# Retention heads and a routed MoE on one core: the load of k, its cast, and the order of 1956 operations

## The chip, the core and the metric

One core of one Trainium2 chip runs the whole program. The metric is device time in microseconds (us) of one execution, lower is better. TensorE is called PE below, VectorE DVE, ScalarE ACT, GpSimd POOL and SyncE SP, as in the profile.

## What is computed

Eight batches of eight heads, 576 positions, head size 64. The scores are masked by a decay that is a power of the distance; the outputs of all heads form 4608 rows of 512, which a router sends to two of eight experts each.

```python
scores = scale * np.matmul(q, k.transpose(0, 1, 3, 2))
Dmat = np.where(rel >= 0, gamma[:, None, None] ** rel[None, :, :], 0.0)
ret = scores * Dmat[None, :, :, :]
x = np.matmul(ret, v)                      # rows of 512 after a transpose
noisy_logits = x @ w_gate + np.log1p(np.exp(x @ w_noise)) * noise
top2 = np.argpartition(-noisy_logits, 2, axis=1)[:, :2]
out[mask] += top2_w[mask, k, None] * (np.maximum(x[mask] @ w1[e], 0.0) @ w2[e])
```

All inputs and the output are f32; the matmuls run in bf16.

## The kernel before, in words

**Units.** The attention part is cut into 16 units (`NU`), each of four heads (`hq`) of one batch (`b` within the pair `bp`), for the first 512 positions. The last 64 positions of a pair of batches are the tail (`load_tail` L652, `tail` L827). For a unit, `load` (L621) issues the DMAs of k, q and v; `cast` (L663) scales q (L676) and v (L683) by the decay tables on DVE or POOL and writes bf16; `tr` (L692) transposes K (L710) and Q (L704) on PE and has ACT or DVE copy them out of PSUM (helper `copy`, L450 on ACT, L452 on DVE); `scores` (L717) multiplies (L736) and masks on DVE (L744); `states` (L751) forms k times v per block (L769), copied by ACT into `tb`; `out_` (L784) adds both parts (L804, L814) and writes xT. After each fourth unit come a tail and `route` (L895): logits (L922), top 2 by a chain of small DVE operations, ranks (L985, L987), a table of row numbers (L1036), and the rows of x with their weights stored to the DRAM buffer xd (L1072).

**How k arrives.** In `load`, k is taken by a DMA that POOL issues (L647, `nc.gpsimd`), which casts f32 to bf16 on the way, into the class of buffers `kb`: eight bf16 pieces of the SBUF tile `ws[2]` that will hold expert 2's weights later. q comes as f32 on SP's queue (L635) into four pieces of `ws[1]` (class `wq`), v as f32 on SP's queue into `big`. K's transposes and the states read the k buffer directly, through `keys` (L689).

```python
go = nc.gpsimd if n == "k" else nc.sync
...
pl.cls("kb", [(ws[2][:, i * F:(i + 1) * F], None) for i in range(8)])
pl.cls("wq", [(ws[1][:, 2 * i * F:2 * (i + 1) * F].bitcast(F32), None) for i in range(4)])
```

The router's two weight matrices and the noise (`later`, L581) are issued on ACT's queue at the program's start (L589, L602, L606).

**Experts.** Weights of experts 0, 1 and 2 are cast by DMAs that POOL issues (L1112, L1116); those of the others come as f32 on SP's queue into `big` and are cast by ACT or DVE (L450, L452). Experts 1 and 2 share memory with q and k, so their weights wait until these buffers are done with. Rows of an expert are gathered from xd in tiles of 128 by POOL (L1179). 15 tiles can start before the last route, from the rows that the first three routes have filled; they go through `up` (L1261, 256 columns at a time) and `second` (L1349) and are called early tiles here. The other tiles wait for the fourth route; they go through `wide` (L1287, up to 512 columns) with the second layer of the tile before woven in (L1349). ReLU (L1270, L1272) and the scaling by the router's weight (L1397 on ACT, L1399 on DVE) empty PSUM; POOL scatters the rows to the output (L1405). For the wide tiles a small DVE copy takes the weight and the row number out of the gathered rows (L1212, `pl`).

**What sets the order.** `record` lists all operations with what they read and write. `Plan.run` (L274) then goes through them with a greedy rule: among the operations whose buffers and inputs are there, it takes the one with the smallest key of planned start, priority and number; where two engines can do an operation it chooses by planned end. The priorities are those of the code plus an entry of the table `ORDER` by name and stage. Each engine executes its instructions in the order that results. For PE's planned idle time in the attention part, `run` puts in matmuls without use (`warm`, L458).

```python
key = (round(t * 20), o.prio, o.i)
if pick is None or key < pick[0]:
    pick = (key, o, e, t, c, taken)
```

## Time and profile before

| what | value |
|---|---|
| three runs | 417.48, 423.11, 436.01 us (median 423.11) |
| profiled execution | 420.08 us |
| its span, first to last instruction | 418.5 us |
| busy over the span | PE 378.8, DVE 166.6, ACT 255.2, POOL 302.1 us |
| bytes moved by DMA | read 72.97 MB, written 26.36 MB |
| first scores (L736) | 13.41 us |
| last scores (L736) | 134.90 us |
| fourth route table (L1036) | 166.69 us |
| first wide matmul (L1287) | 193.28 us |
| PE's last wide and second-layer work | about 409.5 us |

The span has two halves. Up to about 193 us PE works on attention, routes and early tiles; after it on the wide tiles alone. "Busy" is the time in which an engine executes something; PEclk is the share of TensorE's full clock that was granted; the DMA share adds up the time of the packets of 16 DMA engines, and passes 1 where two queues have packets in flight on one engine at a time.

### The profile page before, as it was taken

The numbers are of one execution on the slowest core, as the hardware profiler recorded it, in microseconds if no ns is written. First come the engines' busy times: TensorE is split into PE (matmuls) and PEld (weight loads), VectorE is DVE, ScalarE is ACT, GpSimd is POOL, SyncE is SP. The second block draws the span as 40 slices with busy tenths as digits, with TensorE's granted clock in tenths as the row PEclk, the third lists the DMA queues.
The fourth block names the chain that finished last, engine by engine and source line by source line (L and its number), as shares of the span: only waits on it lengthen the run. The fifth ranks groups of instructions, "written<-read, shape, count | busy, mean of one in ns | idle before, by whom it ended". The sixth has DMA issues, their size and how long they took to land. (4 is left out here: it accounts for less than half of the span.)

```text
span 418.5 us, 11275 instructions
## 1 busy us (share of the span) xinstructions
PE 378.8 (91%) x4415; PEld 235.4 (56%) x4415; DVE 166.6 (40%) x512; ACT 255.2 (61%) x432; POOL 302.1 (72%) x333
## 2 busy tenths in 40 slices
PE   5779786959989889999999999999999999999991
PEld 2457665837768667775566544544554554454461
DVE  5856578694979959220224322113112101100001
ACT  1437676746778765555567777756675676554550
POOL 8997766696399746776577767787786687753882
PEclk9999899697999969999999999999999999999997
DMA  9998999999995999579999999999999999991894
GB/s 219 266 235 189 259 228 186 296 260 257 256 231 107 257 237 254 151 177 238 243 342 383 270 259 279 239 278 223 289 236 232 183 268 182 214 152 25 130 127 105
DMA packets 112584, 93.75 MB, mean 224 GB/s; under 512 B 65807, under 2 KB 89872, under 8 KB 112530
## 3 DMA queue, kind: packets, MB, share of 16 engines
q0 software_dynamic: 34512, 40.31, 52.5%
q1 hardware_dynamic: 75330, 52.53, 49.5%
q8 instruction: 35, 0.57, 0.6%
q10 hardware_dynamic: 2688, 0.18, 0.5%
q14 instruction: 19, 0.16, 0.2%
HBM read 72.97 MB, written 26.36 MB: 237 GB/s over the span
## 5 line engine op out<-in xcount | busy, mean ns | idle before, releaser
L1349 PE MATMUL ps<-W,half 128*128 128x512 bf16 x568 | 185.1, 381 | 0.0
L1287 PE MATMUL ps<-big,W 128*128 128x512 bf16 (+4 forms) x640 | 180.6, 329 | 0.0
L1270 ACT ACTIVATE half<-ps 128x512 bf16<-128x512 f32 (+5 forms) x186 | 93.1, 506 | 77.0 <-PE ps L1287 64.0
L1179 POOL DMA_INDIRECT xg<-xd,xi x80 | 84.9, 1061 | 36.8 <-issue 15.0
L1405 POOL DMA_INDIRECT out_dram<-half,pl x59 | 79.8, 1352 | 28.4 <-ACT half L1270 13.9
L1287 PEld LDWEIGHTS <-W 128*128 128x128 bf16 x640 | 62.6, 98 | 48.7 <-issue 1.0
L1349 PEld LDWEIGHTS <-half 128*128 128x128 bf16 x568 | 55.2, 98 | 60.3 <-issue 0.6
L1212 DVE COPY pl<-xg 128x3 f32<-128x3 f32 (+1 forms) x65 | 13.4, 207 | 117.6 <-DMA xg<-xd,xi 117.5
L744 DVE TENSOR_TENSOR half<-ps,mask 128x512 bf16<-128x512 f32 x64 | 40.4, 683 | 16.0 <-PE ps L736 9.9
L450 ACT ACTIVATE half<-ps 128x1024 bf16<-128x1024 bf16 (+1 forms) x36 | 35.0, 992 | 14.5 <-PE ps L1201 6.0
L683 POOL TENSOR_TENSOR half<-big,tab 128x512 bf16<-128x512 f32 x30 | 31.9, 1080 | 7.2 <-DMA big<-in_v_dram 4.4
L450 ACT ACTIVATE W<-big 128x1024 bf16<-128x1024 f32 x34 | 35.5, 1051 | 0.0
L1261 PE MATMUL ps<-half,W 128*128 128x256 bf16 (+1 forms) x288 | 31.1, 263 | 0.1
L450 ACT ACTIVATE tb<-ps 64x512 bf16<-64x512 f32 x32 | 18.9, 592 | 18.3 <-PE ps L769 18.1
L1397 ACT ACTIVATE half<-ps,pl 128x512 f32<-128x512 f32 x42 | 28.7, 682 | 0.1
L1399 DVE TENSOR_SCALAR half<-ps,pl 64x256 f32<-64x256 f32 (+1 forms) x21 | 11.9, 570 | 39.3 <-PE ps L1368 21.3
L1405 POOL DMA_INDIRECT out_dram<-half,xg x15 | 15.4, 1026 | 16.7 <-ACT half L1397 11.5
L1261 PEld LDWEIGHTS <-W 128*128 128x128 bf16 x288 | 24.6, 101 | 4.7 <-issue 0.2
L676 POOL TENSOR_TENSOR half<-W,tabq 128x1024 bf16<-128x1024 f32 x11 | 20.9, 1903 | 5.4 <-DMA W<-in_q_dram 4.4
L450 ACT ACTIVATE xT<-ps 128x512 bf16<-128x512 f32 (+1 forms) x39 | 19.7, 555 | 6.2 <-PE ps L885 4.2
L458 PE MATMUL ps<-mask,ident__61 128*128 128x512 bf16 x67 | 18.3, 403 | 5.2 <-DVE wgn L592 5.2
L769 PE MATMUL ps<-half,W 64*64 64x64 bf16 (+2 forms) x512 | 18.8, 220 | 3.1 <-issue 2.4
(181 smaller groups left out, 425.1 us busy)
## 6 DMA issues: line engine op xcount, KB each, us to landing
big<-in_moe_w_dram SPq DMA_DIRECT2D x40, 512.0 KB
W<-in_q_dram SPq DMA_DIRECT2D x32, 256.0 KB
big<-in_v_dram SPq DMA_DIRECT2D x14, 512.0 KB
W<-in_moe_w_dram POOLq DMA_DIRECT2D x12, 512.0 KB, 13.0
xd<-xg SPq DMA_DIRECT2D x16, 264.0 KB
W<-in_k_dram POOLq DMA_DIRECT2D x14, 256.0 KB, 10.2
xg<-xd,xi POOLq DMA_INDIRECT x80, 7.2
big<-in_v_dram SPq DMA_DIRECT2D x4, 256.0 KB
```

Source lines behind the costliest of these rows:

```text
L450: self.nc.scalar.activation(out, in_, Act.Copy)
L676: self.eng(e).tensor_tensor(o, i, tabq.t[:, 2 * hq:2 * hq + 2].unsqueeze(3).to_broadcast([P, 2, 8, HD]), Alu.mult)
L683: self.eng(e).tensor_tensor(o, i, t, Alu.mult)
L744: nc.vector.tensor_tensor(S.t.bitcast(BF16).rearrange("p (h c x) -> p h c x", h=2, c=2)[:, h], p[h].t.rearrange("p (c x) -> p c x", c=2), ...
L769: nc.tensor.matmul(o[h * HD:(h + 1) * HD, hp, n, :], lhsT=self.keys(kn, hq, c, r, 2 * hp + h)[:k], rhs=vv[:k, r, c, y].unsqueeze(1).to_bro ...
L1179: ins = nc.gpsimd.indirect_dma_start(out=x.t[:n, :], out_offset=None, in_=self.xd[:rows, :], in_offset=IOff(ap=xi.t[:n, h:h + 1], axis=0), ...
L1261: nc.tensor.matmul(pv()[:, f2, :], lhsT=w.t[:, o:o + P], rhs=xv()[:, di, :n], start=(di == 0), stop=(di == KD - 1))
L1270: self.nc.scalar.activation(o, i, Act.Relu)
L1287: self.mm = nc.tensor.matmul(p.t[:, :n], lhsT=w.t[:, o:o + P], rhs=xv()[:, di, :n], start=(di == 0), stop=(di == KD - 1))
L1349: self.mm = self.nc.tensor.matmul(po.t, lhsT=hv[:, c:c + P], rhs=self.W[e].t[:, o:o + DM], start=(f == 0), stop=(f == KF - 1))
L1397: nc.scalar.activation(y.t[:n, c], x, Act.Copy, scale=g()[:n])
L1405: ins = nc.gpsimd.indirect_dma_start(out=self.out[:, :], out_offset=IOff(ap=ix()[:n], axis=0), in_=y.t[:n, :], in_offset=None, bounds_chec ...
```

## The change

k is loaded as f32 on SP's queue like q and v. It goes, like q, into a class `raw` of eight f32 pieces of `ws[1]` and `ws[2]`, and from unit 12 on into `big`. ACT then casts it to bf16 into a buffer `kn` of the class `half` (two activations of 128x512 per unit), in the layout that v has; K's transposes become 8 of 128x128 per unit instead of 16 half-width ones, and the states read `kn`. The router's matrices and the noise are issued on SP's queue, after the first load of unit 2. The factor 0.125 goes into the exponential of the table `tab` instead of a DVE operation. The greedy rule and `ORDER` are gone: `PLAN` lists all 1956 operations one by one with the engine of each (d DVE, a ACT, p POOL), and `run` only assigns buffers in that order. The planned costs of several operations are other numbers, which now only set the amount of warm-up matmuls and the choice of buffers.

```diff
-        key = (round(t * 20), o.prio, o.i)
-        if pick is None or key < pick[0]:
-            pick = (key, o, e, t, c, taken)
...
+PLAN = """
+9 16 11 12 8 4 126 80p 30 1 14 72p 17 21 18 20 13 22 15 78p 144 127 145 27 69 123p 115d 5 99p 19 23 24 28 26 96p 2 7 3 10 100d 25 45 48 39 37 38 154
...
+        for x in PLAN:
+            o = self.ops[int(x.rstrip("dap"))]
+            e = {"d": "DVE", "a": "ACT", "p": "POOL"}.get(x[-1]) or list(o.eng)[0]
...
-        pl.cls("kb", [(ws[2][:, i * F:(i + 1) * F], None) for i in range(8)])
-        pl.cls("wq", [(ws[1][:, 2 * i * F:2 * (i + 1) * F].bitcast(F32), None) for i in range(4)])
+        pl.cls("raw", [(x[:, 2 * i * F:2 * (i + 1) * F].bitcast(F32), None) for x in ws[1:] for i in range(4)])
...
-            self.raw = {"k": [pl.buf("kb", "att") for c in range(2)], "v": [pl.buf("big", "att") for c in range(2)]}
+            self.raw = {"k": [pl.buf("raw", "k") if u < 12 else pl.buf("big", "k") for c in range(2)], "v": [pl.buf("big", "att") for c in range(2)]}
...
-                go = nc.gpsimd if n == "k" else nc.sync
...
+                got.append(self.inp(lambda e, s=s, t=t, c=c, m=m: nc.sync.dma_start(
...
+        def k(e, c):
+            i = rk[c].t.rearrange("p (h r d) -> p h r d", h=E, r=2)[:, hs]
+            o = bf(kn).rearrange("p (r c h d) -> p c h r d", r=2, c=2, h=4)[:, c]
+            if e == "ACT":
+                nc.scalar.activation(o, i, Act.Copy)
...
+            pl.op({"ACT": 0.63}, 0, lambda e, c=c: k(e, c), r=[(rk[c], hq)], w=[(kn, c)], prio=u + 0.75, port=True)
...
-                        for h in range(2):
-                            nc.tensor.transpose(v[h * HD:(h + 1) * HD, y, x, :], self.keys(s, hq, x // 2, x % 2, 2 * y + h), ident.t)
+                        nc.tensor.transpose(v[:, y, x, :], i[:, 2 * (x % 2) + x // 2, y * P:(y + 1) * P], ident.t)
...
-                pl.op("ACT", 0.55, lambda e, b=b, k=k: nc.scalar.dma_start(
+                pl.op("SP", 0.6, lambda e, b=b, k=k: nc.sync.dma_start(
...
-                    w=[(nz, (b, k))], prio=-6.5, dma=0.2)
+                    w=[(nz, (b, k))], prio=3, dma=0.2, after=self.loads[2][:1])
```

What the new order moves is shown at three places. The first is POOL at the start of the attention part, around its first casts of v (`half<-big,tab`). Before:

```order
L1022 MEMSET pay_206 128x9x5
L647 DMA W_124<-in_k_dram 128x8x128
L683 TENSOR_TENSOR half_94<-big_77,tab 128x4x2x64
L647 DMA W_124<-in_k_dram 128x8x128
L531 MEMSET ltri 128x128
L532 AFFINE_SELECT ltri<-ltri 128x128
L683 TENSOR_TENSOR half_94<-big_77,tab 128x4x2x64
L683 TENSOR_TENSOR half_96<-big_78,tab 128x4x2x64 x2
```

Now, at POOL's casts of q (L534) and v (L541) in the changed kernel:

```order
L371 AFFINE_SELECT mask<-mask 64x128
L534 TENSOR_TENSOR half_91<-W_124,tabq 128x2x8x64
L380 MEMSET ltri 128x128
L541 TENSOR_TENSOR half_95<-big_78,tab 128x4x2x64
L421 MEMSET early 128x1
L541 TENSOR_TENSOR half_96<-big_78,tab 128x4x2x64
L421 MEMSET early 128x1
L421 MEMSET bnd 128x1
L421 MEMSET early 128x1
```

The issues of k between the casts are gone from POOL; casts and small memsets remain.

The second place is the head of SP's queue. Before:

```order
L647 DMA big_77<-in_v_dram 128x4x128
L635 DMA W_123<-in_q_dram 64x2x512 x2
L647 DMA big_77<-in_v_dram 128x4x128
L635 DMA W_123<-in_q_dram 64x2x512 x2
L647 DMA big_77<-in_v_dram 128x4x128 x2
L635 DMA W_123<-in_q_dram 64x2x512 x2
L647 DMA big_78<-in_v_dram 128x8x128 x2
L635 DMA W_123<-in_q_dram 64x2x512 x4
```

Now (L495 loads k and v, L484 q):

```order
L495 DMA W_123<-in_k_dram 128x4x128 x2
L484 DMA W_123<-in_q_dram 64x2x512 x2
L495 DMA big_77<-in_v_dram 128x4x128 x2
L495 DMA W_123<-in_k_dram 128x4x128 x2
L484 DMA W_123<-in_q_dram 64x2x512 x2
L495 DMA big_77<-in_v_dram 128x4x128 x2
L495 DMA W_124<-in_k_dram 128x8x128 x2
```

k leads each unit's loads on SP's queue; q of units 2 and 3 no longer runs far ahead.

The third place is DVE in the part of the wide tiles. Before, around the copies of weights and row numbers (`pl<-xg`):

```order
L1399 TENSOR_SCALAR half_101<-ps_127,pl_149 128x512
L1212 COPY pl_139<-xg_111 128x3
L1212 COPY pl_144<-xg_115 128x3
L1212 COPY pl_134<-xg_117 128x3
L1272 TENSOR_SCALAR half_83<-ps_127 128x192
L1212 COPY pl_135<-xg_112 64x3
```

Now, at the first wide tiles (L1064 is the copy, L1124 the ReLU, L1251 the scaling):

```order
L1124 TENSOR_SCALAR half_99<-ps_128 128x512
L1124 TENSOR_SCALAR half_90<-ps_126 128x2x128
L1064 COPY pl_133<-xg_115 128x3
L1124 TENSOR_SCALAR half_89<-ps_125 128x512
L1124 TENSOR_SCALAR half_100<-ps_126 128x512
L1064 COPY pl_134<-xg_113 128x3
L1064 COPY pl_135<-xg_111 128x3
L1064 COPY pl_136<-xg_113 128x3
```

Many ReLUs have moved from ACT to DVE, behind and between these copies: of the ReLUs over 128x512, 54 are DVE's now and 1 was; ACT has 52 and had 106. Casts of weights for experts 3 to 7 are 25 on ACT and 15 on DVE, after 34 and 6. PE's list has 52 warm-up matmuls where it had 67. The first route table stands after the scores of seven and a half units, where it stood after those of nine; at the last scores PE has done 40 first-layer matmuls of early tiles instead of 56, and between the last scores and the fourth table there are 152 matmuls of early tiles instead of 128.

533 lines of the change are left out of this document (265 added, 268 removed), and 151 rows, old and new, of the table ORDER.

## Prediction

> **What bounds the kernel now.** I read the table of stages first: busy time of each engine, granted clock and DMA share between events of PE's timeline (the first early tiles at about 100 us, the last scores at 135, PE full from 157, the first wide matmul at 193, PE's end at 409.5).
>
> ```profile
> core 0: us, PE busy (x) PEld busy (x) DVE busy (x) ACT busy (x) POOL busy (x), PEclk, DMA share, GB/s
> 0.00:100.00 100.00, 74.49 (x1692) 55.92 (x1693) 68.95 (x237) 55.23 (x85) 79.20 (x131) 0.92 1.16 236
> 100.00:135.00 35.00, 32.53 (x799) 25.96 (x801) 28.26 (x63) 27.75 (x46) 25.08 (x28) 1.00 0.96 214
> 135.00:157.00 22.00, 18.85 (x335) 14.71 (x334) 16.70 (x49) 15.47 (x28) 13.46 (x19) 0.84 1.13 245
> 157.00:193.00 36.00, 36.00 (x325) 25.33 (x322) 15.09 (x45) 19.59 (x37) 25.87 (x27) 1.00 0.76 192
> 193.00:409.50 216.50, 216.50 (x1279) 113.39 (x1277) 36.76 (x117) 137.19 (x239) 156.61 (x131) 1.00 1.05 229
> 409.50:418.50 9.00, 0.41 (x4) 0.12 (x2) 0.88 (x2) 0.00 (x0) 1.93 (x2) 0.76 0.34 97
> ```
>
> ```profile
> 134.90 0.42 PE L736 MATMUL ps<-half,half 64*64 64x128 bf16 x16
> ```
>
> ```profile
> 193.28 0.92 PE L1287 MATMUL ps<-big,W 128*128 128x448 bf16 x4
> ```
>
> From 157 us PE never rests and its clock is whole. The wide part has the same matmuls in both kernels, and so has the last stage, where the last rows are scattered: their 225.5 us stay. What can change is the date of the first wide matmul, 193 us, and that is PE's work before it plus PE's losses. After 100 us the losses are small: 35.00 - 32.53 = 2.5 us idle, then 22.00 - 18.85 = 3.15 us idle and 0.16 of 18.85 = 3.0 us to the lower clock, 8.6 in all. Before 100 us PE is idle for 25.5 us, and part of its busy time is the warm-up matmuls, 18.3 us:
>
> ```profile
> L458 PE MATMUL ps<-mask,ident__61 128*128 128x512 bf16 x67 | 18.3, 403 | 5.2 <-DVE wgn L592 5.2
> L647 POOL DMA_DIRECT2D W<-in_k_dram x18 | 16.1, 895 | 0.3 <-issue 0.3
> L710 PE MATMUL ps<-ident__61,W 128*64 128x128 bf16 x256 | 11.8, 238 | 2.3 <-DMA W<-in_k_dram 2.3
> L704 PE MATMUL ps<-ident__61,half 128*128 128x128 bf16 x128 | 10.3, 226 | 0.6 <-POOL half L676 0.6
> L837 ACT ACTIVATE half<-half 128x512 bf16<-128x512 f32 x4 | 2.5, 633 | 0.7 <-DMA half<-in_k_dram 0.7
> ```
>
> Why PE starves there is the DMA: its share is 1.16 over 100 us. Two stretches of 2 us show what the engines can carry, one nearly all k (q0), one all v (q1).
>
> ```profile
> DMA packets 1248, 0.42 MB, mean 208 GB/s; under 512 B 1113, under 2 KB 1213, under 8 KB 1247
> ...
> q0 software_dynamic: 1104, 0.28, 142.8%
> ```
>
> ```profile
> DMA packets 1190, 0.61 MB, mean 307 GB/s; under 512 B 19, under 2 KB 1180, under 8 KB 1190
> ...
> q1 hardware_dynamic: 1188, 0.61, 115.3%
> ```
>
> The packets per stretch agree (1248 and 1190) while the bytes do not: the engines are limited by packets. PE's lower clock follows its rests, here around 148 us:
>
> ```profile
> 144.00:148.00 4.00, 2.42 (x79) 0.99 1.18 251
> 148.00:152.00 4.00, 2.50 (x15) 0.50 1.12 257
> 152.00:156.00 4.00, 4.00 (x32) 0.66 1.17 220
> ```
>
> **The change, part by part.** *k's transfer.* Now a packet writes 256 B of bf16 (0.28 MB by 1104); as f32 it is one of 512 B, as v's are (0.61 MB by 1188), and there are as many of them.
>
> ```profile
> W<-in_k_dram POOLq DMA_DIRECT2D x14, 256.0 KB, 10.2
> ...
> W<-in_k_dram POOLq DMA_DIRECT2D x4, 128.0 KB, 6.4
> ```
>
> 14 x 256 + 4 x 128 KB are 16384 packets of 256 B. At 2 us / 1248 = 1.60 ns of the sixteen engines they take 26.3 us, at 2 us / 1190 = 1.68 ns 27.5 us: 1.3 us more of DMA time in the attention part. I take it as nothing, since the issue at the head of SP's queue starts k earlier by about as much; the bounds are 0 and +1.3.
> The Trainium skill (DMA: Bandwidth & Descriptors, Specifications) says that a transfer needs at least 512 B for line rate and is a read-modify-write below that. By it k's old packets would cost clearly more than the new ones. The two stretches above do not agree: packets of 256 B pass at least as fast.
>
> *SP's queue.* An issue takes 1.27 / 2 = 0.64 us:
>
> ```profile
> 119.62 1.27 SPq L658 DMA_DIRECT2D half<-in_q_dram  x2
> ```
>
> 18 loads of k and 8 small ones are added to some 75 issues before 126 us, 26 x 0.64 = 17 us in a queue that now spends its time waiting for free buffers and landings. Cover: 126 - 75 x 0.64 = 78 us of such waits; price 0, up to 17 if SP turned out to be the limit, which the DMA share of 1.16 speaks against.
>
> *POOL.* 16.1 us of issues go. Before 100 us POOL is the fullest engine (79.20), and in the first 40 us more so:
>
> ```profile
> 0.00:20.00 20.00, 12.34 (x175) 6.89 (x176) 14.27 (x84) 6.92 (x9) 17.99 (x61) 1.00 1.17 239
> 20.00:40.00 20.00, 16.79 (x424) 12.02 (x424) 11.53 (x34) 9.70 (x16) 18.36 (x21) 1.00 1.14 218
> ```
>
> Where it hurts is seen at 18.7 us: two issues stand before and between POOL's casts of v,
>
> ```profile
> 18.68 0.90 POOL L647 DMA_DIRECT2D W<-in_k_dram  x1
> 19.64 1.05 POOL L683 TENSOR_TENSOR half<-big,tab 128x512 bf16<-128x512 f32 x1
> 20.64 0.94 POOL L647 DMA_DIRECT2D W<-in_k_dram  x1
> ```
>
> while PE fills its time with warm-up until the states of that unit can run:
>
> ```profile
> 19.98 4.49 PE L458 MATMUL ps<-mask,ident__61 128*128 128x512 bf16 x20
> 24.41 1.01 PE L769 MATMUL ps<-half,W 64*64 64x64 bf16 x32
> ```
>
> The gain on the path is at least the 0.90 + 0.94 = 1.8 us of these two, at most the eight issues before 22 us, 8 x 0.895 = 7.2 us; behind 100 us PE does not wait for POOL. After POOL the landing of the inputs is late next, and it is near its limit already, so I take half of the upper end, -3.6.
>
> *ACT.* 32 casts of 128x512 are added, by the row of L837 0.633 us each, 20.3 us. Up to 135 us ACT has 135 - 55.23 - 27.75 = 52 us of idle time, so they are hidden, above all before 100 us. The thin place is 100 to 135 us, where ACT is busy for 27.75 of 35 us: about a third of the casts, 6.8 us, would fill it, but the order hands some copies of K, Q, xT and the states to DVE there. Bounds 0 and +4; I take 0.
>
> *PE.* K's 256 transposes (11.8 us) become 128 like Q's (10.3 us): -1.5 us in a row that PE must work off anyway.
>
> *The order.* It is what can touch the 8.6 us lost between 100 and 157 us, and the rest before. The first route table comes one and a half units earlier in PE's list, and between the last scores and the fourth table stand 152 matmuls of early tiles instead of 128: more to fill the waits of the last route, whose rest around 148 us costs the clock as well. Bounds 0 and -8.6; half of it, -4.3, because each route still is a chain of small DVE operations, and 24 more matmuls are some 4 us of cover.
>
> *The wide part.* DVE takes over about half of ACT's ReLUs. PE is full there and waits for neither, so this is 0, with the risk of the third rival. A second price is on POOL: nine more casts of weights go to DVE, and the trace shows what such a cast can do to a gather, of which 80 take 1061 ns on average:
>
> ```profile
> L1179 POOL DMA_INDIRECT xg<-xd,xi x80 | 84.9, 1061 | 36.8 <-issue 15.0 <-PE ps L1287 7.4 <-PE ps L1368 4.4
> ...
> L452 DVE CAST W<-big 128x1024 bf16<-128x1024 f32 x6 | 4.0, 688 | 0.0
> ```
>
> ```profile
> 284.60 2.14 POOL L1179 DMA_INDIRECT xg<-xd,xi  x1 [0.81 <-PE ps L1368]
> ```
>
> ```profile
> 285.33 1.28 DVE L452 CAST W<-big 128x1024 bf16<-128x1024 f32 x2
> ```
>
> The gather took 1.1 us longer beside two casts (1.28 us). Nine times 0.688 are 6.2 us on POOL, which has 216.5 - 156.6 = 60 us to spare there: 0 on the path, 6.2 if that cover were gone.
> The Trainium skill (SBUF — State Buffer, SBUF: two separate sides) says the same: a copy of this kind on DVE locks GpSimd out of a shared port, and descriptors of its DMAs wait. The trace agrees by the 2.14 us.
>
> **Sum.** -3.6 (POOL) -1.5 (PE) -4.3 (order) = -9.4 us on a span of 418.5, so 409.1; with the 420.08 - 418.5 = 1.6 us around the span 410.7, say **411 us**. The profiled execution's 420.08 lies between the two lower of the three runs (417.48, 423.11), so it stands for an ordinary run, and the median is its upper neighbour.
>
> **Rivals.** *The inputs set the pace (417).* If the attention part ends when the last inputs land, POOL's time is worth nothing, and the order saves only part of the waits: -1.5 and -2 of the 8.6. For it: DMA share 1.16 over 100 us and the same packets afterwards. Against it: between 100 and 157 us PE is the fullest engine, and the last scores at 134.90 come well after the last loads.
>
> *Everything comes in (403).* The upper ends: -7.2 -1.5 -8.6 = -17.3. For it: the losses before 193 us, 8.6 and 25.5 + 18.3 before 100 us, are larger still. Against it: four routes in a row cannot all be covered by tiles that wait for their weights. By the skill's rule on packets under 512 B, taken as a mechanism, k's 26.3 us would halve, 13 us more room for the inputs; it has a part of this case's chance, and as much of the gain before 100 us would give about 400.
>
> *DVE's queue stalls the wide part (430).* DVE waits for the gathers at the copies of weights:
>
> ```profile
> DVE pl L1212 <- DMA xg<-xd,xi: 117.5, 52, 7.4
> ```
>
> Now nothing that PE needs soon is behind them; in the new order ReLUs are. A wait delays PE once it outlasts the free PSUM buffers, some two steps of eight matmuls of 512 columns, about 3.4 us. The row has 52 waits of 2.3 us on average, 7.4 at most. If six of them pass 3.4 us, by 2 us each on average, and such waits come back in the new order, PE loses 12 us, and the kept gains of the attention part vanish with a lower clock after each rest: 420 + 12 - 2 = 430. Against it: the gathers run several tiles ahead, so the order can leave more distance.
>
> *The change does not do what it says:* k might be late behind q and v on one queue, and ACT wait for it in front of its PSUM copies. k stands first in each unit, so this has little chance and would end within 2% of before.
>
> **How the numbers follow.** Chances: forecast 0.44, inputs 0.23, everything 0.18, DVE's queue 0.13, k late 0.02. The forecast's own range is its bounds about halved, 406 to 416. The range **401 to 424** takes in the inputs' case and the upper ends and leaves out the stalled DVE and a little below. About 2% is what a measurement of this kernel can tell from no change: faster by more is below 411.7 against 420.08. That is a little over half of the forecast's case (0.25) and nearly all of the third (0.17) with 0.02 of the second: 0.44. Slower by over 2% is most of DVE's case, 0.11; within 2% the rest, 0.45.
>
> **What would show it.** Right: the first wide matmul at 184 us or so (193 - 9), the wide part still about 216 us with PE full; no L647-like issue on POOL and its casts of v before 22 us; packets of 512 B at about 1190 in 2 us while k loads; ACT's casts near 0.63 us with ACT under 33 of 35 us before the last scores; fewer windows below full clock. Wrong: a first wide matmul at 190 or later (inputs), or a wide part of over 222 us with waits of DVE's copies in front of ReLUs and PE idle (DVE's queue), or ACT waiting on DMA at the casts for more than a few us.

## The result: 442.97 us after 420.3, and the profile after

The changed kernel took 442.97 us (median of 437.52, 442.64, 443.30 and 451.39), the kernel before on the same chip 420.3 us (415.34, 417.48, 423.11, 436.01). An execution that took over 1.5% longer than the fastest of its kernel on that chip is left out of the ratios, intervals and medians from here on, unless the text says otherwise, and n is the number that remain. The ratio is 1.0625, its 95% interval 1.0469 to 1.0781: slower, where 411 us was predicted with a range of 401 to 424.

The profiled execution took 442.64 us, its span is 441.1 us. This is its table of stages, cut at the same events as the one of before, with the columns of that one.

```profile
core 0: us, PE busy (x) PEld busy (x) DVE busy (x) ACT busy (x) POOL busy (x), PEclk, DMA share, GB/s
0.00:100.00 100.00, 70.37 (x1507) 52.55 (x1508) 66.70 (x210) 58.14 (x95) 63.56 (x121) 0.88 1.00 262
100.00:135.00 35.00, 30.74 (x786) 24.82 (x788) 33.48 (x85) 30.71 (x53) 25.38 (x27) 1.00 0.91 235
135.00:157.00 22.00, 18.97 (x364) 14.80 (x364) 19.61 (x57) 14.34 (x28) 13.02 (x19) 1.00 1.13 242
157.00:193.00 36.00, 31.99 (x295) 24.11 (x298) 14.92 (x38) 13.72 (x24) 11.17 (x15) 0.95 0.45 110
193.00:207.05 14.05, 8.63 (x38) 3.70 (x38) 2.78 (x10) 1.95 (x3) 10.70 (x12) 0.88 0.64 142
207.05:428.90 221.85, 216.29 (x1256) 113.66 (x1280) 89.44 (x229) 83.12 (x141) 158.25 (x134) 1.00 1.01 230
428.90:441.10 12.20, 0.06 (x1) 0.00 (x0) 0.48 (x1) 0.00 (x0) 4.37 (x4) 0.59 0.55 97
```

Before, PE was busy for all of 157 to 193 us (36.00 of 36.00), and the wide part began there. Now PE is busy for 31.99 of these 36 us, the DMA share falls from 0.76 to 0.45, POOL is busy for 11.17 us instead of 25.87, and 14 more us pass before the wide part begins. The events that cut the stages, from PE's timeline of the changed kernel (start, duration, what ran, and in brackets the idle time before it and who ended it):

```profile
136.51 0.61 PE L588 MATMUL ps<-half,half 64*64 64x128 bf16 x16
...
154.08 0.24 PE L837 MATMUL ps<-MM,ltri 128*128 128x144 bf16 x1 [0.61 <-DVE MM L810]
...
171.38 1.20 PE L888 MATMUL ps<-oh,olo 128*128 128x80 f16 x18 [3.80 <-DVE oh L883]
...
195.74 5.18 PE L1201 MATMUL ps<-W,half 128*128 128x512 bf16 x16 [2.71 <-DVE half L1124]
...
207.05 2.43 PE L1139 MATMUL ps<-big,W 128*128 128x448 bf16 x12 [2.67 <-DMA big<-xg]
```

L588 are the scores, L837 the ranks of the fourth route, L888 its table, L1139 the first layer of the wide tiles; L1201 is a second layer. So the time went here (an event is the start of its row; PE's last matmul is counted to its end):

| stretch | before, us | after, us | difference |
|---|---|---|---|
| start to the last scores | 134.9 | 136.5 | +1.6 |
| last scores to the fourth route table | 31.8 | 34.9 | +3.1 |
| route table to the first wide matmul | 26.6 | 35.7 | +9.1 |
| first wide matmul to PE's last one | 216.6 | 221.9 | +5.3 |
| PE's last one to the end of the span | 8.6 | 12.1 | +3.5 |

They add up to the 22.6 us between the spans. Over half of it, 12.2 us, lies between the last scores and the wide part. From the route table to the first wide matmul, first before and then after, the stretch reads, in the columns of the table of stages:

```profile
166.69:193.28 26.59, 26.59 (x243) 18.85 (x241) 6.12 (x27) 14.76 (x28) 19.43 (x19) 1.00 0.67 173
171.38:207.05 35.67, 30.09 (x222) 19.83 (x227) 8.88 (x28) 8.53 (x13) 12.12 (x13) 0.90 0.41 90
```

Of the 9.1 us, 5.6 are idle time of PE, which had none before; the other 3.5 are busy time, at a granted clock of 0.90 where it was 1.00. In this stretch POOL's timeline shows one large hole:

```profile
170.81 0.99 POOL L1257 DMA_INDIRECT out_dram<-half,xg  x1 [0.31 <-issue]
192.01 1.04 POOL L1031 DMA_INDIRECT xg<-xd,xi  x1 [20.20 <-PE ps L1201]
193.35 0.98 POOL L1031 DMA_INDIRECT xg<-xd,xi  x1 [0.30 <-issue]
```

POOL had a gather of the wide tiles (L1031) to issue and stood for 20.20 us until a second-layer matmul (L1201) of an early tile was done. The rows of this and the following gathers thus arrive after 192 us. DVE gets them at 194.93, and PE waits for them (the 2.71 and 2.67 us above).

```profile
194.93 0.17 DVE L1064 COPY pl<-xg 128x3 f32<-128x3 f32 x1 [5.35 <-DMA xg<-xd,xi]
195.01 1.28 DVE L1124 TENSOR_SCALAR half<-ps 128x512 bf16<-128x512 f32 x2
```

Here a ReLU on DVE (L1124) does stand behind a copy that waits for a gather (L1064), as the prediction's third rival had it; but the gather is late because of POOL's wait. A second hole is in the last route's chain, on DVE and on ACT at the same time:

```profile
160.15 0.18 DVE L864 TENSOR_SCALAR ps<-ps 128x18 int32<-128x18 int32 x1
164.38 0.18 DVE L866 TENSOR_SCALAR hi<-ps 128x18 int32<-128x18 int32 x1 [4.05 <-ACT ps L870]
```

```profile
163.88 0.38 ACT L1122 ACTIVATE half<-ps 128x256 bf16<-128x256 f32 x1 [0.65 <-PE ps L1113]
164.16 0.18 ACT L870 ACTIVATE ps<-vals 128x18 f32<-128x18 f32 x1
```

DVE waits 4.05 us for a copy of 0.18 us on ACT (L870), which stands behind ACT's ReLUs. The copy writes another part of the same PSUM tile that DVE's next step (L866) reads; DVE needs nothing of it. From the ranks to the table it takes 17.3 us, where it took 10.2 (156.47 to 166.69).

### The profile page after: what moved, and what is told of

Read it like the earlier page. It is cut to its first block, busy times and chain, and to the rows that moved or that the text cites. A ratio compares the mean times of both kernels' runs of the same rounds, so it can differ in the third digit from the quotient of the medians.

```text
span 441.1 us, 10948 instructions
## 1 busy us (share of the span) xinstructions
PE 377.1 (85%) x4238; PEld 233.6 (53%) x4272; DVE 227.4 (52%) x626; ACT 202.0 (46%) x340; POOL 286.5 (65%) x327
## 4 chain that ended last, share of the span: by engine, by line
PE 53%; DMA 15%; issue 10%; DVE 9%; SPq 5%; POOL 4%; ACT 3%; POOLq 0%; DVEq 0%; ACTq 0%
PE ps L1139 21%; PE ps L1201 19%; DMA big<-in_moe_w_dram 5%; DMA out_dram<-half,pl 3%; PE ps L1113 3%; DVE half L596 3%; PE ps L305 2%; SPq L484 2%; DMA W<-in_k_dram 2%; DMA big<-in_v_dram 2%; PE ps L1220 2%; DMA xg<-xd,xi 1%; PE ps L588 1%; DMA noise<-in_moe_noise_dram 1%; POOL half L534 1%
## 5 line engine op out<-in xcount | busy, mean ns | idle before, releaser
L1201 PE MATMUL ps<-W,half 128*128 128x512 bf16 x542 | 181.4, 382 | 5.0 <-DVE half L1124 2.7
L1139 PE MATMUL ps<-big,W 128*128 128x512 bf16 (+4 forms) x632 | 178.8, 328 | 4.7 <-DMA big<-xg 2.7
L1031 POOL DMA_INDIRECT xg<-xd,xi x80 | 82.8, 1035 | 57.0 <-PE ps L1201 23.7
L1124 DVE TENSOR_SCALAR half<-ps 128x512 bf16<-128x512 f32 (+5 forms) x104 | 57.1, 563 | 96.1 <-PE ps L1139 74.7
L1122 ACT ACTIVATE half<-ps 128x512 bf16<-128x512 f32 (+5 forms) x92 | 44.4, 504 | 105.8 <-PE ps L1139 79.5
L1139 PEld LDWEIGHTS <-W 128*128 128x128 bf16 x640 | 62.5, 98 | 51.5 <-issue 4.5
L1201 PEld LDWEIGHTS <-half 128*128 128x128 bf16 x568 | 55.3, 99 | 65.0 <-issue 6.9
L1249 ACT ACTIVATE half<-ps,pl 128x512 f32<-128x512 f32 (+1 forms) x37 | 23.3, 639 | 34.1 <-PE ps L1201 19.4
L297 ACT ACTIVATE half<-ps 128x1024 bf16<-128x1024 bf16 (+1 forms) x31 | 30.3, 997 | 11.8 <-PE ps L557 6.4
L541 POOL TENSOR_TENSOR half<-big,tab 128x512 bf16<-128x512 f32 x29 | 30.5, 1063 | 7.7 <-DMA big<-in_v_dram 7.1
L297 ACT ACTIVATE W<-big 128x1024 bf16<-128x1024 f32 x25 | 25.9, 1053 | 9.0 <-DMA big<-in_moe_w_dram 9.0
L534 POOL TENSOR_TENSOR half<-W,tabq 128x1024 bf16<-128x1024 f32 x10 | 19.0, 1900 | 9.3 <-DMA W<-in_q_dram 4.9
L1251 DVE TENSOR_SCALAR half<-ps,pl 128x512 f32<-128x512 f32 (+1 forms) x26 | 17.7, 684 | 13.5 <-PE ps L1201 9.4
L1064 DVE COPY pl<-xg 128x3 f32<-128x3 f32 (+1 forms) x65 | 9.8, 179 | 27.5 <-DMA xg<-xd,xi 27.5
L588 PE MATMUL ps<-half,half 64*64 64x128 bf16 x512 | 15.0, 231 | 10.0 <-ACT xg L297 6.4
L1257 POOL DMA_INDIRECT out_dram<-half,im x12 | 15.7, 1307 | 7.1 <-DVE half L1124 3.8
L1257 POOL DMA_INDIRECT out_dram<-half,xg x15 | 15.3, 1022 | 7.3 <-issue 3.3
```

Of the source, the lines that this page charges most:

```text
L297: self.nc.scalar.activation(out, in_, Act.Copy)
L534: self.eng(e).tensor_tensor(o, i, tabq.t[:, 2 * hq:2 * hq + 2].unsqueeze(3).to_broadcast([P, 2, 8, HD]), Alu.mult)
L541: self.eng(e).tensor_tensor(o, i, t, Alu.mult)
L1031: ins = nc.gpsimd.indirect_dma_start(out=x.t[:n, :], out_offset=None, in_=self.xd[:rows, :], in_offset=IOff(ap=xi.t[:n, h:h + 1], axis=0), ...
L1122: self.nc.scalar.activation(o, i, Act.Relu)
L1124: self.nc.vector.tensor_relu(o, i)
```

## Theory and rivals

**What the new list changes besides the order on each engine.** The instructions of all engines are emitted in one sequence, that of PLAN, and two kinds of waits hang on this sequence and not on the five lists taken apart. The first is a tie that the program makes by hand. A gather of the wide tiles waits for the last matmul of an expert that was emitted before it (`self.mm`), so that gathers go at PE's pace:

```python
if pace:
    self.tc.add_manual_dep(ins.ins, self.mm.ins.name, mybir.DependencyInfo(
        mybir.DependencyClass.Sync, mybir.DependencyReason.DATA), reason="gathers go at TensorE's pace")
```

The second is any wait that the framework puts in between two accesses of one tile, in the sequence of emission. The greedy rule emitted nearly in order of planned time: no operation follows one planned over 9.4 us later, and no gather is tied to a matmul whose planned end lies more than 1.6 us behind the gather's own planned start. In the new list the planned time steps back some 700 times, by up to 29.8 us. By its own plan the first paced gather belongs at 157.5 us, but it stands in the list behind a matmul planned to start at 173.7, so it is tied to that one. Counted to the planned end of the matmul, the first five ties are 16.6, 13.8, 10.0, 7.1 and 5.3 us late. In the same way L870 stands in the list between L864 and L866.

*Theory:* these ties and waits make the loss. *Rivals:* the ReLUs behind copies on DVE's queue (the prediction's third rival); the new head of the program, where PE's first scores come 5.5 us later; the inputs, with k as f32; and the place of a drain on POOL, because of which scatters are left over at the end.

The tool that tells the first two apart is a sort of the list of operations before they are emitted. Sorting by planned time leaves every engine's own list as it is, since on one engine planned times only grow. It changes only the sequence across engines, and with it the waits that follow from this sequence, both kinds at once.

## Experiments: the sequence of emission

### The whole list in order of planned time, the ties alone, the copy of L870 alone

Four kernels on one chip, where before had 431.76 us (n = 1). The first sorts the whole list.

```diff
         assert len(order) == len(self.ops)
+        order.sort(key=lambda x: x[1])
```

> The changed kernel with every engine's list unchanged, instruction by instruction; only the operations are emitted sorted by their planned start, so that each paced gather is tied to the matmul that is planned beside it (the first one to PE's matmul 2722 instead of 2944). Theory A (the ties are too late, because the new list is not in order of time): POOL's wait of 20.2 us before the gather at 192.0 is gone, the first wide matmul comes at 198 to 202 instead of 207, the wide part takes 217 to 219 us instead of 222, in all 430 to 435 against 442.6. Theory B (the ReLUs behind DVE's copies of weights, or the buffers of the gathers, hold PE whatever the ties are): the same gathers wait for something else, 440 to 445.

Measured: 440.73 us (n = 1; 447.8 is the median of all four, 445.9 that of all seven of the kernel before). The changed kernel did not run on this chip, and chips differ, so these times do not say what the sort gained. They do show that it harmed the head. The warm-up matmuls read the decay mask as their operand, and now POOL's work on it is emitted first. From the timeline of this kernel:

```profile
16.43 4.92 PE L305 MATMUL ps<-mask,ident__61 128*128 128x512 bf16 x15 [5.73 <-POOL mask L371]
```

The first scores came at 26.3 us (18.9 in the changed kernel), the last at 144.2, in an execution of 448.1 us. The sort moved more than the two waits in question; a later one spares the head.

The second kernel takes the tie away, the third does the same to the kernel before.

```diff
-                if pace:
+                if False:
```

> The changed kernel without the tie of the gathers to TensorE's pace; all lists unchanged. The gathers are then held by their buffers, their row numbers and POOL's own order alone. Theory A: as a_sorted or a little better, 428 to 435; more gathers may lie beside the loads of weights. Theory B: 440 to 445.

Measured: 469.5 us (n = 3; 467.2 to 470.2), the slowest time here. The gathers are no longer held, but the wide part took 249 us in the profiled execution (479.0 us), where the sorted kernel on the same chip took 226 (in its 448.1 us), with waits like this one in PE's timeline and the one of DVE that ended it:

```profile
372.23 0.59 PE L1139 MATMUL ps<-big,W 128*128 128x512 bf16 x1 [8.02 <-DVE half L1124]
```

```profile
371.49 0.69 DVE L1124 TENSOR_SCALAR half<-ps 128x512 bf16<-128x512 f32 x1 [10.94 <-remote]
```

What held DVE for 10.94 us the trace does not name ("remote"); POOL issued without a break from 345 to 372 us at that time. So the kernel needs something that holds its gathers, and taking the tie away says nothing on what a late one costs.

> The control: the kernel before without the tie of the gathers to TensorE's pace. Its list is in order of planned time, so the ties lie within 1.6 us of the planned start of each gather. Theory A: they cost next to nothing there, within 1% of before (416 to 424). If the ties cost much in any order, this is faster by 2% or more.

Measured: 437.8 us (n = 2) beside 431.8 (n = 1); the medians of all executions are 442.1 and 445.9. So the times of the kernel before do not tell what its tie is worth. In this profile the first wide matmul comes at 207.9 us, where it came at 193.3 in the profile of the kernel before on the first chip.

The fourth kernel has DVE make the copy of L870, so that DVE does not wait for ACT.

```diff
-        o("ACT", 0.22, lambda e: nc.scalar.activation(val(), self.fixed["vals"].t.rearrange("p (j c) -> p j c", j=2), Act.Copy),
+        o("ACT", 0.22, lambda e: V.tensor_copy(val(), self.fixed["vals"].t.rearrange("p (j c) -> p j c", j=2)),
```

> The changed kernel with one small copy of each route (L870, 128x18) on DVE at its place in the list instead of on ACT. Theory C (in the fourth route DVE waits 4.05 us for this copy, which stands on ACT behind ReLUs that wait for PE): the wait and most of PE's rest of 3.8 us before the fourth table are gone, the fourth table comes at 167 to 168 instead of 172.4, and as all that follows hangs on PE, the end moves by 3 to 6 us: 437 to 440. Rival: the chain is held by the other small operations or by early tiles between them, and the end stays within 1%: 440 to 445.

Measured: 462.2 us (n = 4; 459.9 to 464.9). The row of L866 shows that the wait is gone:

```profile
163.78 0.18 DVE L866 TENSOR_SCALAR hi<-ps 128x18 int32<-128x18 int32 x1
```

From the ranks to the table it took 15.0 us (155.8 to 170.8), where the changed kernel took 17.3. But the total is above every time of the changed kernel on other chips, with a wide part of 243 us, and no copy of the changed kernel ran on this chip. A wait shown gone, a total without an explanation: all that this run gives is the 2.3 us in the route, and those against another chip.

### Sorted from 150 us on

Now the head stays as it is, and only what is planned after 150 us, the last route and all that follows, is sorted. The same chip ran the changed kernel itself and two more versions.

```diff
         assert len(order) == len(self.ops)
+        order.sort(key=lambda x: max(x[1], 150.0))
```

> The changed kernel itself, once more, as the standard for the others of this set on the same chip. All theories: slower than the kernel before by about 6% (5 to 8%).

> The changed kernel, every engine's list unchanged; from 150 us of the plan on, the operations are emitted in order of planned time, so that the gathers are tied to the matmuls planned beside them; everything before is as it was. Theory A (late ties): 2 to 4% faster than a_ctl: no wait of some 20 us on POOL, the first wide matmul 5 to 8 us sooner, fewer waits in the wide part. Rival: the same as a_ctl within 1%, because the gathers are held by something else.

Measured: the changed kernel 444.4 us (n = 4; 443.6 to 450.1), sorted 432.0 (n = 4; 430.1 to 435.2): 12.4 us or 2.8% less, with not one instruction moved on any engine. From POOL's timeline, first the changed kernel on this chip, then the sorted one, and from the sorted kernel's timeline of DVE:

```profile
190.79 1.04 POOL L1031 DMA_INDIRECT xg<-xd,xi  x1 [20.22 <-PE ps L1201]
```

```profile
172.43 1.03 POOL L1031 DMA_INDIRECT xg<-xd,xi  x1 [4.07 <-PE ps L1201]
```

```profile
158.74 0.18 DVE L866 TENSOR_SCALAR hi<-ps 128x18 int32<-128x18 int32 x1
```

The first paced gather waits 4.07 us instead of 20.22, and L866 waits for nobody (4.05 us in the changed kernel, here too). In the sorted kernel the table starts at 166.0 us and the first wide matmul at 192.8; in the changed kernel on this chip at 170.2 and 205.2. So 4.1 us came back up to the table and 8.3 from there to the wide part, together as much as the medians differ. The stretch from table to wide part, first in the changed kernel and then in the sorted one:

```profile
170.15:205.20 35.05, 30.23 (x222) 19.77 (x227) 9.16 (x28) 8.53 (x13) 11.48 (x13) 0.90 0.40 89
166.02:192.80 26.78, 26.57 (x223) 18.32 (x228) 9.67 (x32) 8.61 (x14) 17.81 (x18) 1.00 0.83 173
```

With the waits PE's idle time is gone (4.8 us, now 0.2), and its clock is whole: nearly the same matmuls keep it busy for 3.7 us less. After that the wide part is 1.8 us shorter and the tail 3.1 longer (16.5 us after 13.4), which will be the drain's matter below. The theory holds for the stretch before the wide part; the sort changes ties and framework waits together, and only the two rows above tell them apart.

### DVE's queue, and the head

On the same chip: the sorted kernel with all ReLUs of the wide tiles (the function at line 1152) on ACT, which is the third rival undone.

```diff
         for o, t in order:
-            o.fn(o.on)
+            o.fn("ACT" if o.fn.__code__.co_firstlineno == 1152 else o.on)
```

> As a_s150, with all ReLUs of the wide tiles on ACT, as nearly all were before; the copies of weights and row numbers stay on DVE. Theory D (ReLUs in DVE's queue behind copies that wait for gathers stall PE): the wide part is back to 216 to 218 us without waits of PE for ReLUs, 1 to 3% faster than a_s150. Rival (the gathers themselves come too late for PE): the waits move from L1124 to the transposed rows, and the time stays within 1% of a_s150.

Measured: 430.6 us (n = 3; 429.6 to 431.7) beside 432.0: no difference. Where the gathers come in time, the ReLUs that moved to DVE cost nothing; as a cost of its own the rival is out there.

And the changed kernel, unsorted, without the 14 warm-up matmuls that stand before K's first transposes, and with warm-ups that read the identity instead of the mask. It undoes this chain at the head of the changed kernel, in one timeline of all engines:

```profile
4.89 4.61 PE L305 MATMUL ps<-mask,ident__61 128*128 128x512 bf16 x14 [4.89 <-POOL ident__61 L363]
...
9.98 0.69 DVE L299 COPY half<-ps 128x1024 bf16<-128x1024 bf16 x1 [4.21 <-PE ps L563]
...
11.14 0.32 ACT L356 ACTIVATE tab<-tab,ln 128x32 f32<-128x32 f32 x1 [5.66 <-DVE tab L352]
```

PE spends 4.61 us on warm-up, K's transposes (L563) wait behind it, DVE's copy of K waits for them, the decay table on ACT waits for DVE, and the scaling of v and of q stands behind the tables.

```diff
-            if o.fill:
+            if o.fill and o.i != 154:
...
-            self.nc.tensor.matmul(b.t, lhsT=ident, rhs=mask.rearrange("p r x -> p (r x)").unsqueeze(1).to_broadcast([P, 2, 2 * P]),
+            self.nc.tensor.matmul(b.t, lhsT=ident, rhs=ident.unsqueeze(1).to_broadcast([P, 4, P]),
```

> The changed kernel without the 14 warm-up matmuls ahead of the first K transposes, and with the other warm-ups reading the identity instead of the mask that POOL is still writing. Theory E (the start is held by a ring: warm-ups, K's transposes, DVE's copy, the tables behind it, q's cast): the first scores come at 13 to 15 us instead of 18.9, and the last scores 3 to 5 us sooner, 1% faster than a_ctl. Rival (the inputs set the pace of the attention part): the first scores come sooner, the last at the same time, and the end within 0.5% of a_ctl.

Measured: 445.9 and 448.2 us (n = 2) beside 444.4 (n = 4): not faster. The first scores came at 16.3 us instead of 20.2, the last at 135.3 instead of 136.2. Of 3.9 us won at the head, 0.9 is left 120 us later. The profile of the new one is of an execution of 452.9 us, longer than the two counted, so somewhat more than 0.9 may have been left in those; but their times show no gain either. Little or nothing of a gain at the first scores reaches the end of the attention part.

## Experiments: what is left

### The drain on POOL, and the load alone

POOL has one operation that is there to wait until its outstanding transfers are done, the drain (L1536 before, L1388 after). In the list of before, 3 scatters and a read of output rows stand between the last gather and the drain, and 17 issues after it, reads and scatters together; in the new list 12 scatters and 28 issues. A hole of 9.55 us in POOL's timeline marks it in both kernels. Before:

```profile
383.05 1.55 POOL L1405 DMA_INDIRECT out_dram<-half,pl  x1 [9.55 <-ACT half L1270]
...
411.16 0.98 POOL L1405 DMA_INDIRECT out_dram<-half,pl  x1 [0.71 <-DVEq L1548]
```

After:

```profile
386.74 1.55 POOL L1257 DMA_INDIRECT out_dram<-half,pl  x1 [9.55 <-DVE half L1251]
...
433.17 1.02 POOL L1257 DMA_INDIRECT out_dram<-half,pl  x1 [0.30 <-issue]
```

Before, the last scatter starts 1.3 us after PE's end (409.91), and POOL has rested for 0.71 us. Now it starts 4.2 us after PE's end (428.96) with "issue" before it: POOL still works off a backlog, one scatter per 1.86 us. On a further chip, where before took 433.7 us (n = 4): the sorted kernel with L870 on DVE, and the same with the drain (operation 1947) moved to 4 scatters behind the last gather.

```diff
-        order.sort(key=lambda x: max(x[1], 150.0))
+        order.sort(key=lambda x: 333.5 if x[0].i == 1947 else max(x[1], 150.0))
```

> As a_s150 (ties in order of planned time from 150 us on), and the small copy of each route (L870) on DVE at its place in the list instead of on ACT. Theory C (DVE's wait for this copy behind ACT's ReLUs lengthens the fourth route): the step from the ranks (L837) to the fourth table (L888) shrinks by about 4 us against a_s150, the first wide matmul comes 2 to 4 us sooner, the ratio to before falls from 1.007 to 1.000 or a little below. Rival (with the ties mended the early tiles cover the route): the table comes sooner, the first wide matmul does not, and the ratio stays within 0.5% of a_s150.

> As a_sv, with POOL's drain four scatters after its last gather instead of twelve; all else unchanged. Theory F (after PE's end POOL still works off scatters, since the drain behind a row of scatters held it 15.6 us): the drain takes about 9.6 us as in the kernel before, the scatters end 5 to 6 us sooner, 1.0 to 1.4% faster than a_sv. Rival (POOL has the same number of scatters left either way and is the limit by their sum): within 0.3% of a_sv.

Measured: 444.6 us (n = 3; ratio to before 1.0277, 1.0104 to 1.0450) and 433.5 (433.4 and 433.6, n = 2). From PE's end to the end of the span it took 16.3 us without and 12.2 with the drain moved. The rest of the 11 us between them lies before the wide part (the first wide matmul at 208.2 and 201.1 us), where the two kernels are alike, so only the 4.0 us of the tail are to be put down to the drain; the 7.1 us show how far two profiles of the same instructions on one chip can lie apart. L870 on DVE brought nothing beyond the sort (ranks to table 15.3 us, sorted alone 13.6 on another chip), as it must if the sort has already taken that wait away.

The load alone: the kernel before with its greedy rule, and of the change only k as f32 on SP's queue, the cast on ACT and K's transposes of full width.

```diff
-                go = nc.gpsimd if n == "k" else nc.sync
+                go = nc.sync
...
+        for c in range(2):
+            pl.op({"ACT": 0.63}, 0, lambda e, c=c: k(e, c), r=[(rk[c], hq)], w=[(kn, c)], prio=u - 1, port=True)
```

> The kernel before with its greedy rule and its table, and the change of the load alone: k as f32 on SP's queue (into four f32 pieces where eight bf16 pieces were), cast by ACT, K's transposes over the whole width, noise and gates left on ACT's queue. The greedy rule places the new operations with a table that was not made for them. Theory G (the load itself is neutral, what was lost was lost by the written order): 0.98 to 1.02 of before, with a wide part of 216 to 218 us. Rival (the load costs: one queue for all inputs, four pieces of k instead of eight): 1.02 to 1.05, with the last scores 4 us later or more.

Measured: 439.9 us (n = 3), ratio 1.0126 with an interval of 0.9904 to 1.0348: the total is not told apart from before. The sign that was named for the rival is there, though: the last scores came at 143.7 us, where the kernel before on the first chip had 135.1, both counted to the start of the very last one.

Then the sorted kernel with half of k: from unit 6 on the load leaves out the upper half of each packet, so that a packet carries 256 B instead of 512. If the inputs limit by bytes, the scores come earlier.

```diff
+                    in_=s[m, 256 * c:256 * c + 256].rearrange("h (p r) d -> p h (r d)", r=2)) if n == "v" or u < 6 else nc.sync.dma_start(
+                    out=t.t.rearrange("p (h x) -> p h x", h=E)[:, m, :HD], in_=s[m, 256 * c:256 * c + 256].rearrange("h (p r) d -> p h (r d)", r=2)[:, :, :HD]),
```

> As a_s150, but from unit 6 on each load of k brings only half of each packet's row (256 B instead of 512 B, as many packets); the other half is what an earlier load left, so the output is not the reference's. If the engines are limited by packets in the attention part, the last scores stay at 135 to 137 us; if by bytes, they come 3 to 5 us sooner; the stages behind are those of a_s150 either way.

Measured: 450.5 us (n = 1). The last scores came at 140.3 us; the two sorted kernels above on the same chip had 142.0 and 138.8. The stretch of 100 to 135 us moved 192 GB/s, where those moved 217 each:

```profile
100.00:135.00 35.00, 31.22 (x760) 25.13 (x757) 31.90 (x78) 27.95 (x47) 25.45 (x27) 0.95 0.73 192
```

The DMA share is 0.73, and 0.84 and 0.83 in those two, and yet the scores lie between theirs. One execution, beside two that are alike up to there and 3.2 us apart, does not exclude the 3 to 5 us that were expected if bytes are the limit, but it shows nothing of them.

### All on one chip

The changed kernel, the sorted one, the sorted one with the drain moved, and the kernel before with ties made late, with before itself at 416.6 us (n = 5).

> The changed kernel itself as the standard of this set. 1.035 to 1.065 of the kernel before.

> The ties in order of planned time from 150 us on (as a_s150). Theory A: 2 to 4% faster than c_ctl on the same chip, the first wide matmul 8 to 14 us sooner.

> As c_s150, and POOL's drain four scatters after the last gather instead of twelve. Theory F: the time after PE's end falls from about 16 to about 12 us, 1% faster than c_s150. Rival: within 0.3% of c_s150.

| kernel | us | n | ratio to before, interval | table to first wide, us | PE's end to span's end, us |
|---|---|---|---|---|---|
| changed | 445.9 | 2 | 1.0770 (1.0675 to 1.0865) | 34.9 | 14.2 |
| sorted from 150 us | 428.8 | 4 | 1.0279 (1.0240 to 1.0319) | 26.8 | 15.0 |
| the same, drain moved | 426.7 | 4 | 1.0248 (1.0184 to 1.0312) | 26.8 | 11.1 |

The stages are those of the profiled executions, which took 444.5, 439.0 (one that the 428.8 leaves out) and 425.3 us. The 20 us wait is there again in the changed kernel (20.21 us for PE's L1201). Of its 7.7% the sort alone takes 4.9 points away, with every engine's list unchanged. The sorted kernel is 3.8% under the changed one here, after the 2.8% on the other chip. The drain's move shows on POOL's timeline: the hole comes at 347 us, after four scatters, and is shorter.

```profile
345.54 1.65 POOL L1257 DMA_INDIRECT out_dram<-half,pl  x1 [0.30 <-issue]
353.66 1.59 POOL L1257 DMA_INDIRECT out_dram<-half,im  x1 [6.46 <-issue]
...
414.86 1.02 POOL L1257 DMA_INDIRECT out_dram<-half,pl  x1 [0.30 <-DMA out_dram<-half,pl]
```

The tail is shorter by 3.9 us, and 4.0 on the other chip; in the total it is 2.1 us, with intervals that overlap.

The last one takes the kernel before, keeps every engine's list, and emits POOL's operations after 160 us up to 6 us of planned time later, so that the ties hang on matmuls 36 to 56 later.

```diff
+        order.sort(key=lambda x: max(150.0, x[1] + (min(6.0, max(0.0, x[1] - 160), max(0.0, (360 - x[1]) / 10)) if x[0].on == "POOL" else 0.0)))
```

> The kernel before, every engine's list unchanged; only the ties of its paced gathers are later, by what is planned in 6 us (36 to 56 matmuls further on). Theory A: gathers come 6 us later than the order reckons with, PE waits for rows and ReLUs in the wide part, 1 to 3% slower than before. Rival (gathers run so far ahead that 6 us do not matter, and the new lists are slow for other reasons): within 0.5% of before.

Measured: 419.3 us (n = 1), a ratio of 1.0065; the median of all four is 426.6, that of all nine of the kernel before 418.0. In its profile (an execution of 427.5 us) the first wide matmul is at 192.7 us, as before. Up to 6 us of lateness show no clear cost. In the changed kernel the first tie was 16.6 us late, so this does not answer the theory either way.

### Late ties and the load, once more

The two edits of the kernel before were run again on another chip.

> The change of the load alone under the greedy rule, as b_load. Theory G (the load is neutral): 0.99 to 1.01 of before. Rival (the load costs, by one queue for all inputs): 1.01 to 1.03, with the last scores 5 us later or more than the 135 us of before.

> The kernel before with the ties of its gathers later by what is planned in 6 us, lists unchanged, as b_late. Theory A: 1.01 to 1.03 of before, by a longer wide part and later scatters at the end. Rival (the gathers run far enough ahead): 0.995 to 1.005.

Measured: the load alone 440.2 us (n = 4), the late ties 437.6 (n = 5); before had 428.9 with n = 1, and the median of all its eleven executions there was 441.9, of all six of each of the two kernels 441.2 and 438.2. Against the single execution they are 1.026 and 1.020, by the medians of all there is no difference. It stays open whether the load alone costs a per cent. But the named sign of the rival came again, now beside a kernel with the old load on the same chip: the last scores at 144.1 us with the new load, at 138.3 in the kernel with late ties. Under the greedy rule, then, the attention part ended some 6 us later in these profiles; whether by the new load or by what the greedy rule makes of it (its priorities were not made for the new operations) no run tells.

No version ran faster than the kernel before.

## Why the prediction was wrong

**The order (-4.3 predicted, +12.2 measured).** The step that failed is "It is what can touch the 8.6 us lost between 100 and 157 us", with bounds of 0 and -8.6. Most of the loss lies outside these 8.6 us, in the stretch from 157 us to the wide part where PE had never rested. The step read the new order as five lists, one per engine, and asked only which work stood where on an engine. The cost lay in what the lists do not show: what a gather was tied to (20.20 us of POOL's time) and between which two accesses of one tile a third had been emitted (4.05 us of DVE's). To PE's idle time came its lower clock behind it (0.90 of full from the table to the wide part). The sort, which leaves the lists as they are, took 12.4 us away on one chip and 17.1 on another. A bound of 0 on the costly side had no reason behind it: that a list is permuted across engines does not exclude a loss. The tie itself was in the code of both kernels, in the function that issues the gathers.

**The wide part and the tail ("their 225.5 us stay", now 234.0).** That "PE is full there and waits for neither" was the second step to fail: the matmuls keep PE busy for as long as before (216.35 us after 216.63), but it is idle for 5.6 us where it never was. The 3.5 us of the tail are POOL's: its drain stands behind 12 scatters instead of 3 and a read, and the last scatter starts 4.2 us after PE's end instead of 1.3. Moving the drain took about 4 us off the tail on two chips. The prediction had set POOL's spare time in this part, 60 us, against its work as a whole, and not asked how much of the work was left at the end. The other 5.3 us are in part settled. The largest wait in PE's row, 2.45 us at 254.67 us, ends with a ReLU on DVE, and that stood behind a cast of weights on DVE (L299), one of 15 there where 6 were before, which waited for its weights:

```profile
253.52 0.69 DVE L299 CAST W<-big 128x1024 bf16<-128x1024 f32 x1 [6.66 <-DMA big<-in_moe_w_dram]
254.13 0.48 DVE L1124 TENSOR_SCALAR half<-ps 128x320 bf16<-128x320 f32 x1
```

```profile
254.67 0.27 PE L1053 MATMUL ps<-ident__61,xg 64*128 64x64 bf16 x4 [2.45 <-DVE half L1124]
```

The changed kernel has this wait of DVE on all three chips (6.66, 6.44 and 5.33 us), the sorted one on two has none. The prediction had priced these casts only by what they take from POOL. The rest stays open: first wide matmul to PE's end took 216.6 us in the kernel before and 221.9 in the changed one, but 221.1 in the kernel before with late ties (its execution of 427.5 us), 223.4 in the changed one on that chip, and 217.8 in the sorted one with the drain moved.

**POOL's issues (-3.6 predicted).** The issues are gone and POOL is busy for 63.56 us of the first 100 instead of 79.20, but the last scores came 1.6 us later. The first rival had it that time won at the start is worth nothing at the end of the attention part, and the head experiment points the same way (3.9 us at the first scores, 0.9 at the last). The rival's reason, the inputs, was not confirmed: with half of k's bytes nothing came earlier. What sets the pace of that part stays open; with the new load under the greedy rule its end came later still. With its 417 us the first rival too lacked the loss in the order.

**What was right.** PE's -1.5: K's transposes are now the row of Q's.

```profile
L525 ACT ACTIVATE half<-W 128x512 bf16<-128x512 f32 x24 | 14.5, 624 | 10.1 <-DMA W<-in_k_dram 10.0
L563 PE MATMUL ps<-ident__61,half 128*128 128x128 bf16 x128 | 10.3, 221 | 0.8 <-DVE mb L1094 0.6 <-ACT half L525 0.2
L525 ACT ACTIVATE half<-big 128x512 bf16<-128x512 f32 x8 | 4.8, 630 | 0.0
```

ACT's casts take 14.5 + 4.8 = 19.3 us, 20.3 were forecast; between 100 and 135 us ACT is busy for 30.71 us, under the 33 that were named as the sign. ACT did wait for k at the casts, 10.0 us in all, which the prediction had named as a sign of k being late; ACT has idle time there, and K's transposes waited only 0.2 us for a cast. k's transfer came out as forecast:

```profile
DMA packets 1226, 0.66 MB, mean 332 GB/s; under 512 B 40, under 2 KB 1189, under 8 KB 1226
...
q1 hardware_dynamic: 1226, 0.66, 110.5%
```

1226 packets in 2 us, where 1190 were forecast and k's smaller ones had passed at 1248. The Trainium skill (DMA: Bandwidth & Descriptors, Specifications) gives 512 B as the least transfer for line rate, with a read-modify-write below that. The first half agrees with the rates here, 208 GB/s in k's old packets and 332 now; that a smaller packet takes longer by itself is not seen. "Limited by packets" holds for these two sizes only: from 8 to 10 us of the kernel before, 790 larger packets filled the engines as well (0.74 MB, 107.8% in q1 alone). And as 110.5% of one queue shows, a DMA share over 1 does not need two queues. Gathers did not suffer from DVE's larger share of casts (1035 ns on average, 1061 before).

**DVE's queue (the rival of 430 us).** Nearest in time, by luck, since it named another cause: waits of this form are visible (2.71 us and 2.45 us of PE's time behind ReLUs on DVE), but with the order of emission mended and all these ReLUs on ACT the time was the same. Behind the first of them is a late gather, late by its tie; behind the second a cast that waited for weights.

**What stays open.** After the sort and the drain 2.5% are left (1.0248, 1.0184 to 1.0312). The profile places the last scores of that version at 137.6 us and its table at 168.1, 2.7 and 1.4 us later than in before's profile (from another chip), its first wide matmul at 194.8 (193.3), its wide part is 217.8 us (216.6) and its tail 11.1 (8.6): several small pieces, none of them tested by itself. Nor is the length of the stretch from the route table to the wide part explained on some of the chips. It is 26.8 us on two chips once the order of emission is mended, but 33.4 and 31.1 in the two sorted kernels on a third, 33.9 for the kernel before with late ties and 40.9 for it without ties. Whether late ties alone, without the framework's waits, make the loss was not tried on the changed kernel.

## What to carry to other kernels

When a list of operations replaces a scheduler, compare not only each engine's order: for every tie between engines, hand-made or put in by the framework, look at the planned times of its two ends, and emit in order of planned time so that no operation hangs on one that was meant for later. Do that where the loss is, and look at the rest again: over the whole list the sort harmed the head here. An engine with time to spare over a stage can still hold its end; look at what it has left when the bounding engine stops. A gain at the start of a stage is worth only as much as the last event of the stage moves, so try that with one small edit before it is put in a sum.

## What the runs showed of the hardware that was not expected

The same program differs by more between chips than by most edits here: medians of the kernel before were 416.4, 416.6 and 433.7 us on three chips (n = 2, 5 and 4), so that only kernels of one chip may be compared.

The hole at the drain in POOL's timeline depends on where it stands: 6.5 us behind 4 scatters (two chips), 9.55 in the kernel before, behind 3 and a read. Behind 12 scatters it is 9.55, 11.53 and 11.20 us in the changed kernel, and in sorted ones from 11.57 to 16.83. What else it depends on was not tried.

Without the ties the changed kernel took 469.5 us, where the same kernel with ties and a sorted list took 440.7 on that chip. The sort itself was worth 12.4 and 17.1 us on two others, so that some of the 29 us are the missing ties': an engine that issues its transfers as early as it can is not always better than one that waits. In the kernel before the two times, 437.8 without ties and 431.8 with them (n = 1), do not tell.

PE's clock follows its waits: from the route table to the wide part it was granted 0.90 in the changed kernel and 1.00 in the sorted one on the same chip, and nearly the same matmuls (222 and 223 records) kept PE busy for 30.2 and 26.6 us.
